# Folding the transform along d, and moving the w_out conversion into attention, in an attention, gated-mixture and Fourier-mixing kernel

## The chip, the cores and the metric

The kernel runs on one core of a Trainium2 chip. The metric is the device time of one execution in microseconds (us). Engines are called TensorE (PE), VectorE (DVE), ScalarE (ACT), GpSimd (POOL) and SyncE (SP, which only issues DMAs here).

## The reference

Three stages follow each other, for a batch of 2, 768 positions and 8 heads of 64 (512 features):

```
scores = where(bucket(q) == bucket(k), q @ k.T / 8, -1e9)   # buckets: sign bits of q @ proj
x      = softmax(scores) @ v                                # joined to 2 x 768 x 512
gate   = sigmoid(causal convolution of x over 5 positions, by feature)
x      = (gate * (x @ w_val)) @ w_out
mixed  = real(fft(fft(x, axis=1), axis=2))                  # along the sequence, then along d
u      = x + mixed
out    = u + relu(layernorm(u) @ w_ch1) @ w_ch2
```

The weights of the last two stages arrive as 64-bit floats and are read as pairs of 32-bit words.

## The kernel before

Products are kept near float32 precision by splitting each operand into a high and a low part (fp32r) and adding three products, high·high, high·low and low·high. A weight in 64 bits is first turned into such parts by `from64` (L125 to L164): five or six elementwise steps on VectorE and two on ScalarE, 512 columns at a time.

**Attention** (L230 to L819) runs over 8 pairs of heads (p), 12 steps each (i), n = 12 p + i, in the order of one hand-written loop. Each step places scores, softmax, transposes and products with v on TensorE, and beside them preparatory work: the placement of the next pair's q and k by DMA into the buffers q2 and k2, the normalization of the pair before, the conversion of one 256-column half of w_val per pair (`val_weights`, L681, whose intermediates lie in PSUM), and the convolution of finished x on GpSimd (`conv_pool`, L209, in `conv_tmp`). x is stored transposed in xT, one tile per batch. `x_split` (L185) casts a part of it to its high half on ScalarE and subtracts for the low half, on GpSimd by default. At the end of the loop value products (`val_matmul`, L194: 12 matmuls of 384 columns for a tile c of batch b and sequence half a) start: "early" tiles for (0, 0), then "late" ones for (0, 1). `gate` (L205) multiplies a value tile on VectorE with the sigmoid of the convolution.

**Mixing** (L886 to L1075) is what the change rewrites. It first does the 8 value tiles of batch 1 (`val`, L942). In program order between them stands the conversion of w_out, `run(wo[c])` at L960, four calls on 512 columns each, from a load of w_out that is issued behind the last outputs of attention (L910). The convolution of the last feature chunk (1, 3) is on GpSimd, and that of (1, 2) on VectorE (`conv_dve`, L219, at the end of attention).

Gated values g are folded along the sequence by `even_odd` (L926): VectorE adds or subtracts position j and 768 − j (gt), ScalarE casts the high part gh (L929) and GpSimd subtracts for the low part gl (L930). s = 0 is the even, s = 1 the odd part. Then:

- L974: w_out (high and low) is transposed on TensorE, 32 transposes.
- L984: w_out times the DFT table along d (`wide`, cosines and sines, 258 columns each) gives wah and wal: 96 matmuls of 258 columns.
- L1015: gh and gl times wah and wal give ah and al, the transform along d of the block's input x: 84 matmuls of 258 columns for each batch.
- `own` (L1032): gh and gl times w_out itself, 12 matmuls of 512 columns for each of 6 row tiles a batch. Both this and L1015 go through `gmm`, whose matmul is L1003.
- `mixed` (L1037, L1049): the transform along the sequence of ah and al by the tables seq and odd.
- `total` (L1054) adds own and mixed, where the columns from 257 on are the mirrored ones of 255 down to 1; GpSimd adds and subtracts even and odd totals to u (L1073), `center` takes off the mean (VectorE, L863), `u_transpose` (L877, matmul L880) makes the input of the channel stage, and `channel_split` (L857) converts w_ch1 and w_ch2 for it.

**The channel stage** (L1081 to L1163) is a loop of matmuls, L1109 and L1121.

The pool of q2 and k2 is closed with attention. All order is program order on each engine; semaphores join the engines, and a PSUM bank is reused in the order in which its pool gives it out.

Of the kernel before, what the change touches and what calls it, by code (L numbers as in the profile page):

```python
# [10 lines left out]
F32 = mybir.dt.float32  # L11
# [88 lines left out]
def block_kernel(  # L100
# [118 lines left out]
    def conv_dve(c, i):  # L219

        x, dst = xT[1], g[1][:, c, :]
        if i == 0:
            nc.vector.tensor_scalar_mul(dst, x[:, c, 0:S], cwt[:, 0, c : c + 1])
        for kk in (1, 2) if i == 0 else (3, 4):
            nc.vector.scalar_tensor_tensor(
                dst, x[:, c, kk : kk + S], cwt[:, kk, c : c + 1], dst, op0=ALU.mult, op1=ALU.add
            )


    def attention(es):  # L230
        ap1 = pool(es, "ap1")
        ap2 = pool(es, "ap2", 2)
        ap3 = pool(es, "ap3")
# [50 lines left out]
        q2 = [ap3.tile([P, 2, S], F32R, name=f"q2_{i}") for i in range(NBUF)]  # L284
        k2 = [ap3.tile([P, 2, S], F32R, name=f"k2_{i}") for i in range(NBUF)]
# [388 lines left out]
        wv_raw, wv_e = {}, {}  # L674
# [6 lines left out]
        def val_weights(i):  # L681

            c, h = divmod(i, 2)
            cs = slice(h * DM // 2, (h + 1) * DM // 2)
            n = DM // 2
            words = wv_raw[i].bitcast(I32).rearrange("p (n two) -> p n two", two=2)
            lo, hi = words[:, :, 0], words[:, :, 1]
            t = psm.tile([P, 2 * n], F32, tag="m", name="cvp")
            a, g = (t[:, x * n : (x + 1) * n].bitcast(I32) for x in range(2))

# [7 lines left out]
            def step2():  # L698
                nc.scalar.activation(a, a, AF.Relu, scale=8.0, bias=col[:, 3:4])
                e = ap1.tile([P, n], I32, tag="cve", name="cv", bufs=1)  # L700
                nc.vector.scalar_tensor_tensor(a, hi, -(2 ** 31), a, op0=ALU.bitwise_and, op1=ALU.bitwise_or)
                nc.vector.tensor_scalar(e, a, -(2 ** 23), None, op0=ALU.bitwise_and)
                wv_e[i] = e

            def step3():
                nc.vector.scalar_tensor_tensor(
                    wvl[:, c, cs], g, 2.0 ** -35, wv_e[i].bitcast(F32), op0=ALU.mult, op1=ALU.mult
                )

            def step4():  # L710
                nc.scalar.copy(wvh[:, c, cs], a.bitcast(F32))
# [4 lines left out]
        convs = [(b, c, i) for b, c in pairs[: NPR - 2] for i in range(9)]  # L716
        start()
        NT = 12 * NPR
        for n in range(NT + 2):
# [43 lines left out]
            if n == NT - 1:  # L763
# [5 lines left out]
                for c in range(NC):  # L769
                    x_split(0, 1, c)  # L770
# [18 lines left out]
            for _ in range(5 * n // 6 - 5 * (n - 1) // 6):  # L789
                if convs and n < NT and n >= 12 * (4 * convs[0][0] + convs[0][1]) + 22:  # L790
# [11 lines left out]
            if n >= NT:  # L802
                conv_dve(2, n - NT)
                sigmoid(0, 2 * (n - NT))
                sigmoid(0, 2 * (n - NT) + 1)
                if n > NT:
                    for c in range(NC):
                        gate(0, 0, c, tail[c])
        xsplit[1, 0] = xsplit[0, 0]
        late = []  # L810
        for c in range(NC):
            x_split(1, 0, c, nc.vector)
# [5 lines left out]
        for c in range(NC):  # L818
            gate(0, 1, c, late[c])  # L819

# [65 lines left out]
    def mixing(es):  # L886
        mp = pool(es, "mp")
        ps = pool(es, "psx", 8, psum=True)

        def psum():  # L890
            return ps.tile([P, 512], F32, tag="ps", name="ps")

        woh = mp.tile([P, NC, DM], F32R, name="woh")
        wol = mp.tile([P, NC, DM], F32R, name="wol")
        wah = mp.tile([P, NC, 2, NL], F32R, name="wah")
        wal = mp.tile([P, NC, 2, NL], F32R, name="wal")


        ep = pool(es, "ep", 2)
        seq = ep.tile([P, 2, 2, 3, HS], F32R, name="seq", bufs=1)  # L900
        odd = ep.tile([P, 2, P], F32R, name="odd", bufs=1)
        vs = ExitStack()
        vp = pool(vs, "vp", side="right")
        conv_tmp = xT[0].rearrange("p c t -> p (c t)")[:, :S]
        gts = [ep.tile([P, HS], F32, name=f"gt{i}", bufs=1) for i in range(4)]
        rs = ExitStack()
        rp = pool(rs, "rp")
        raws = [rp.tile([P, DM], I64, name=f"wor{c}") for c in range(NC)]
        for c in range(NC):
            nc.sync.dma_start(raws[c], w_out[c * P : (c + 1) * P, :])  # L910
        toh = vp.tile([P, NC, DM], F32R, name="toh")
        tol = vp.tile([P, NC, DM], F32R, name="tol")
        wide = vp.tile([P, 2, NC, 2 * NL], F32R, name="wide")
        xsplit[1, 1] = tuple(vp.tile([P, NC, HS], F32R, name=f"xs{i}") for i in "hl")


        gh, gl = {}, {}

        def parts_tiles(b, pl):
            for s in range(2):  # L920
                gh[b, s] = pl.tile([P, NC, HS], F32R, tag=f"gh{s}", name="gh", bufs=1)
                gl[b, s] = pl.tile([P, NC, HS], F32R, tag=f"gl{s}", name="gl", bufs=1)

# [15 lines left out]
        wo = [from64(rp, raws[c], woh[:, c, :], wol[:, c, :], half=True) for c in range(NC)]  # L939
# [6 lines left out]
        nc.gpsimd.dma_start(wide, t_wide)  # L946
        for i in range(6):
            conv_pool(1, 3, i, conv_tmp)
        for c in range(NC):
            x_split(1, 1, c)  # L950
        for c in range(3):
            sigmoid(1, c)
        for i in range(6, 9):
            conv_pool(1, 3, i, conv_tmp)
        nc.gpsimd.dma_start(seq, t_seq)
        nc.gpsimd.dma_start(odd, t_odd)
        for c in range(NC):
            val(0, c)
        for c in range(NC):
            run(wo[c])  # L960
            val(1, c)
            if c == 3:
                sigmoid(1, 3)
                nc.scalar.activation(warm, warm, AF.Sqrt)
            gate(1, 0, c, pvs[0, c])
        for c in range(NC):
            gate(1, 1, c, pvs[1, c])


        for c in range(NC):  # L970
            for i, (w, to) in enumerate(((woh, toh), (wol, tol))):
                pw = psum()
                for m in range(NC):
                    nc.tensor.transpose(pw[:, m * P : (m + 1) * P], f32(w)[:, m, c * P : (c + 1) * P], ident)  # L974
                nc.scalar.copy(to[:, c, :], pw)
        rs.close()
        pp = pool(es, "pp")
        parts_tiles(0, pp)
        for i, (m, part) in enumerate((m, part) for part in range(2) for m in range(NC)):
            pa = psum()  # L980
            n = 0
            for w, x in ((toh, 0), (toh, 1), (tol, 0)):
                for c in range(NC):
                    nc.tensor.matmul(  # L984
                        pa[:, :NL], w[:, c, m * P : (m + 1) * P], wide[:, x, c, part * NL : (part + 1) * NL],
# [216 lines left out]
```

## Time and profile before

| what | us |
|---|---|
| median of 3 runs (657.67 to 661.81) | 659.42 |
| the profiled execution | 658.59 |
| its span in the trace | 656.8 |
| TensorE busy | 636.2 |
| VectorE busy | 454.3 |
| ScalarE busy | 357.6 |
| GpSimd busy | 275.2 |

The span is what the trace covers, from the first instruction to the last; the execution's time has 1.8 us around it. Busy shares average over stages with different limits, so the reading goes by stretches. Attention lasts to about 257 us, mixing to 380.3, the channel stage to the end.

### The profile page before, as it was taken

How to read it: one execution, taken by the hardware profiler on the slowest of the kernel's cores; microseconds unless marked ns; L12 is line 12 of the kernel's file. 1: busy time of each engine (PE TensorE's matmuls, PEld its weight loads, DVE VectorE, ACT ScalarE, POOL GpSimd, SP SyncE). 2: the span in 40 equal slices, each digit the busy share in tenths (PEclk: the TensorE clock that was granted, in tenths of full speed). 3: DMA queues.
4: the chain of work that ended last, by engine and by line, in shares of the span. 5: the costliest groups of instructions: out<-in, count | busy, mean ns of one | idle time of the engine just before them, and what ended most of it. 6: DMA issues, size and time to landing. Idle time of an engine off the chain costs nothing.

```text
span 656.8 us, 10829 instructions
## 1 busy us (share of the span) xinstructions
PE 636.2 (97%) x3954; PEld 597.1 (91%) x3954; DVE 454.3 (69%) x832; ACT 357.6 (54%) x707; POOL 275.2 (42%) x285
## 2 busy tenths in 40 slices
PE   7999999999999999969999989999999999999997
PEld 6899999999999999869989878999999899999996
DVE  4998999999898987987756478899886511111113
ACT  5888989888798996355313345555665211111110
POOL 7132578788788698925531343333332000000000
PEclk9999999999999999979999999999999999999999
DMA  6957465675755303450000123444441100000002
GB/s 157 202 124 169 128 160 126 145 181 132 188 130 132 92 17 114 153 216 1 1 1 1 54 76 129 128 129 129 128 130 64 70 26 1 0 1 1 0 1 96
DMA packets 54061, 61.32 MB, mean 93 GB/s; under 512 B 28936, under 2 KB 42332, under 8 KB 53752
## 3 DMA queue, kind: packets, MB, share of 16 engines
q1 hardware_dynamic: 53272, 56.02, 32.1%
q0 software_dynamic: 432, 4.60, 1.9%
q8 instruction: 31, 0.51, 0.3%
q14 instruction: 22, 0.18, 0.1%
q10 hardware_dynamic: 304, 0.01, 0.0%
HBM read 35.04 MB, written 3.15 MB: 58 GB/s over the span
## 4 chain that ended last, share of the span: by engine, by line
PE 80%; DVE 11%; POOL 3%; issue 2%; ACT 1%; SPq 1%; DMA 1%; DVEq 0%; POOLq 0%; ACTq 0%
PE pf L1109 19%; PE acc L1121 19%; PE sp L469 8%; PE ps L1003 8%; PE op L529 8%; PE ptp L506 7%; PE ps L1049 2%; PE bp L346 2%; DVE ptl L518 1%; DVE sd L481 1%; PE ptp L601 1%; DVE cv L149 1%; DVE cv L146 1%; PE ps L974 1%; POOL g L217 1%
## 5 line engine op out<-in xcount | busy, mean ns | idle before, releaser
L1121 PE MATMUL acc<-w,hid 128*128 128x512 f32 x576 | 137.1, 390 | 0.0
L1121 PEld LDWEIGHTS acc<-w,hid 128*128 128x128 f32 x576 | 107.4, 188 | 19.8
L1112 DVE SCALAR_TENSOR_TENSOR hid<-pf,hid 128x384 fp32r<-128x384 f32 x60 | 32.2, 555 | 120.0 <-ACT hid L1111 120.0
L481 DVE TENSOR_SCALAR_CACHE_REDUCE sd<-sp 128x768 f32<-128x768 f32 x96 | 91.0, 948 | 16.1 <-PE sp L469 15.2
L518 DVE TENSOR_TENSOR ptl<-ptp,pth 128x768 fp32r<-128x768 f32 x96 | 91.4, 952 | 5.9 <-ACT pth L514 5.9
L1109 PE MATMUL pf<-uth,w 128*128 128x384 f32 x480 | 94.7, 338 | 0.2 <-POOL w L155 0.2
L514 ACT CAST pth<-ptp 128x768 fp32r<-128x768 f32 x96 | 77.3, 805 | 31.0 <-PE ptp L506 13.6
L469 PE MATMUL sp<-k,q 128*128 128x384 f32 x384 | 90.8, 358 | 3.0 <-DVE sd L481 1.7
L488 ACT ACTIVATE sd<-sd,nm 128x768 f32<-128x768 f32 x96 | 90.7, 944 | 2.7 <-DVE sd L481 2.7
L1111 ACT ACTIVATE hid<-pf 128x384 fp32r<-128x384 f32 x60 | 28.0, 488 | 113.9 <-PE pf L1109 113.9
L1109 PEld LDWEIGHTS pf<-uth,w 128*128 128x128 f32 x480 | 85.6, 187 | 3.0 <-POOL w L155 0.5
L155 POOL TENSOR_TENSOR w<-cv 128x512 fp32r<-128x512 f32 x32 | 41.4, 1293 | 107.9 <-DVE cv L150 95.5
L506 PE MATMUL ptp<-ident,sd 128*128 128x128 f32 x576 | 78.6, 273 | 0.2 <-ACT sd L488 0.2
L529 PE MATMUL op<-ptl,v 128*128 128x256 f32 x288 | 73.8, 285 | 0.0
L529 PE MATMUL op<-pth,v 128*128 128x256 f32 x288 | 73.8, 283 | 0.0
L469 PEld LDWEIGHTS sp<-k,q 128*128 128x128 f32 x384 | 62.3, 189 | 6.3 <-DVE sd L481 4.1
L506 PEld LDWEIGHTS ptp<-ident,sd 128*128 128x128 f32 x576 | 65.8, 141 | 1.0 <-ACT sd L488 0.5
L547 POOL TENSOR_TENSOR xm<-xc,xs 64x256 f32<-64x256 f32 x48 | 36.1, 751 | 67.8 <-ACT sd L488 31.6
L142 ACT ACTIVATE cv<-cv,col 128x512 int32<-128x512 int32 (+1 forms) x37 | 26.5, 716 | 57.6 <-DVE cv L139 57.6
L529 PEld LDWEIGHTS op<-ptl,v 128*128 128x128 f32 x288 | 54.7, 190 | 0.9 <-issue 0.2
L529 PEld LDWEIGHTS op<-pth,v 128*128 128x128 f32 x288 | 54.6, 190 | 0.0
L1109 PE MATMUL pf<-utl,w 128*128 128x384 f32 x240 | 52.1, 338 | 0.0
(222 smaller groups left out, 1118.2 us busy)
## 6 DMA issues: line engine op xcount, KB each, us to landing
raw<-in_moe_w_ch_dram SPq DMA_DIRECT2D x32, 512.0 KB, 3.7
q<-ht SPq DMA_DIRECT2D x30, 192.0 KB
k<-ht SPq DMA_DIRECT2D x30, 192.0 KB, 3.1
rqk<-in_q_dram SPq DMA_DIRECT2D x16, 192.0 KB, 3.6
rqk<-in_k_dram SPq DMA_DIRECT2D x16, 192.0 KB, 4.5
rv<-in_v_dram SPq DMA_DIRECT2D x8, 384.0 KB, 3.3
out_dram<-o SPq DMA_DIRECT2D x12, 256.0 KB, 2.1
xs<-xc SPq DMA_DIRECT2D x47, 64.0 KB, 1.9
```

The costliest lines, as they stand in the source:

```text
L155: nc.gpsimd.tensor_tensor(dst_l, fold(g.bitcast(F32)), fold(e.bitcast(F32)), op=ALU.mult)
L469: nc.tensor.matmul(sp[:, a, :HS], q2[i][:, m, qi * P : (qi + 1) * P], k2[i][:, m, a * HS : (a + 1) * HS], start=m == 1, stop=m == 0,)
L481: nc.vector.tensor_scalar(sd[n].rearrange("p (a c) -> p a c", a=2), sp[:, :, :HS], CLAMP, None, op0=ALU.min, op1=ALU.min, accum_out=st[p][ ...
L488: nc.scalar.activation(sd[n], sd[n], AF.Exp, bias=st[p]["nm"][:, i : i + 1], scale=-1.0, accum_out=st[p]["sums"][:, i : i + 1],)
L506: nc.tensor.transpose(tp[:, r // 3, c0 : c0 + P], sd[n][:, r * P : (r + 1) * P], ident)
L514: nc.scalar.copy(p_parts(n)[0], tp)
L518: nc.vector.tensor_tensor(lo, tp, f32(ho), op=ALU.subtract)
L529: nc.tensor.matmul(po[kb], v3[:, r, c0 : c0 + P], pt[kb][x][:, r, :], start=r == 0 and x == 0, stop=r == R - 1 and x == 1,)
L547: add[kb] = lambda: nc.gpsimd.tensor_tensor(st[p]["xm"][mr, blk * QB : (blk + 1) * QB], xc[mr, :], xs[mr, :], op=ALU.add)
L1003: nc.tensor.matmul(dst, x[:, c, m * P : (m + 1) * P], w(c), start=n == 0, stop=n == 3 * NC - 1)
L1109: nc.tensor.matmul(pf[:, :HS], w[:, c, :], x[:, c, cs], start=n == 0, stop=n == 3 * NC - 1)
L1121: nc.tensor.matmul(acc, x[:, ts_], w, start=f == 0 and n == 0, stop=f == NF - 1 and n == 2)
```

## The change

- The transform along d is applied to y = own(x) after it has been formed, not to w_out. VectorE folds y along d: columns d and 512 − d are added (for part 0) or subtracted (part 1), with a fold of 256 columns (`fold`). TensorE transposes the fold, 3 or 2 blocks (`turn`), ScalarE and VectorE split it into high and low parts, and `along_d` multiplies by a table of half the size (`tab`, and `first` for d = 0): 8 or 6 matmuls of 258 columns for each of the 7 parts a batch, 100 in all. L974, L984 and the narrow use of L1003 go. The 12 pairs (b, s, kt) run as passes i = 0 to 13 of one loop, with `own` of pass i, `along_d` of pass i − 2 and `turn` of pass i − 1.
- `total` adds the mixed tile from PSUM straight into y in SBUF.
- w_out is loaded in eight halves of 256 columns during pairs 6 and 7 (`out_load`) and converted by `half_weights` (the code of `val_weights`) into the buffers of q and k, whose pool stays open. Half 0 is converted in the loop, halves 1 to 7 behind it, each in a `begin` (three VectorE steps) and an `end` (ScalarE and three VectorE steps).
- `x_split(0, 0)` goes from pair 7 to pair 5; the subtraction of `x_split(0, 1)` from GpSimd to VectorE; the convolution of (1, 2) from VectorE to GpSimd; the multiplications of (1, 3) from GpSimd to ScalarE (`conv_act`). The sigmoids and gates of (0, 0) come earlier.
- The means of batch 0 (`center`) are placed in passes 8 to 10, the conversions of the first channel weights in passes 9 and 10, the transposes of u in passes 11 to 13.
- PSUM in mixing: 2 banks for `turn` and 6 for the rest, where it was one pool of 8.

The core of the diff:

```diff
-            if p == 7 and i in (1, 3, 5, 7):
+            if p == 6 and i in (2, 6):
+                out_load(i // 6)
+            if last and i == 7:
+                for x in range(2):
+                    out_load(2 + x)
+                    out_tile(x)
+                osteps = out_weights(0, "m")
+            if last and 7 <= i < 11:
+                osteps[i - 7]()
+                if i == 10:
+                    osteps[4]()
+            if p == 5 and i in (1, 3, 5, 7):
                 x_split(0, 0, i // 2)
...
+        begin(1)
+        x_high(1, 0, 0)
+        x_high(1, 0, 1)
+        begin(2)
+        end(1)
+        x_high(1, 0, 2)
+        x_high(1, 0, 3)
+        for c in range(3):
+            x_low(1, 0, c, nc.vector)
+        late_gate(0)
+        end(2)
+        begin(3)
+        x_low(1, 0, 3, nc.vector)
+        late_gate(1)
+        begin(4)
+        end(3)
+        late_gate(2)
+        end(4)
+        begin(5)
+        begin(6)
+        late_gate(3)
+        end(5)
+        end(6)
+        begin(7)
+        end(7)
...
         for c in range(NC):
             x_split(1, 1, c)
+        for c in range(NC):
+            val(0, c)
+        for c in range(2):
             sigmoid(1, c)
+            gate(1, 0, c, pvs[0, c])
+        conv_act(3)
         nc.gpsimd.dma_start(seq, t_seq)
         nc.gpsimd.dma_start(odd, t_odd)
...
+        def fold(b, s, kt, yp):
+            y = ys[b, s, kt] = m2.tile([P, DM], F32, tag="y", name="y", bufs=7)
+            nc.scalar.copy(y, yp)
+            for part in (s,) if s == 0 or kt else (0, 1):
+                fo = folds[b, s, kt, part] = m2.tile([P, 2 * P], F32, tag="fold", name="fold", bufs=2)
+                nc.vector.tensor_tensor(
+                    fo, yp[:, 1:257], y[:, 511:255:-1], op=ALU.subtract if part else ALU.add
+                )
...
+        for i in range(len(jobs) + 2):
+            if i < len(jobs):
+                yp = own(*jobs[i])
+            if i > 1:
+                for x in spans(jobs[i - 2]):
+                    if x[0] not in sums:
+                        sums[x[0]] = [m2.tile([P, 2, 4, NL], F32R, tag=y, name="a") for y in ("ah", "al")]
+                    along_d(*x)
+            if 0 < i <= len(jobs):
+                for x in spans(jobs[i - 1]):
+                    turn(*x)
+            if i == 7:
+                both(0, 0)
+                both(0, 1)
+            if i < len(jobs):
+                fold(*jobs[i], yp)
```

How the order moves at three places. Names: `wor` is a raw piece of w_out, `cvp` its intermediates in PSUM, `qk` its converted parts; `xl`, `xsh` and `xsl` are parts of x of batch 1; g_73 and g_74 are the gates of batch 0 and 1.

VectorE behind the last step of attention, before:

```order
L189 TENSOR_TENSOR xl<-xT_78,xh 128x384 x4
L207 TENSOR_TENSOR g_73<-late,g_73 128x384 x4
L139 TENSOR_SCALAR cv<-wor_3859 128x512
L145 TENSOR_SCALAR cv<-wor_3859 128x512
L146 SCALAR_TENSOR_TENSOR cv<-wor_3859,cv 128x512
```

and after, around the third and fourth of the late gates:

```order
L216 TENSOR_TENSOR g_73<-late,g_73 128x384
L746 SCALAR_TENSOR_TENSOR cvp<-wor,cvp 128x256
L747 TENSOR_SCALAR cv<-cvp 128x256
L750 SCALAR_TENSOR_TENSOR qk<-cvp,cv 128x256
L738 TENSOR_SCALAR cvp<-wor 128x256
L739 TENSOR_SCALAR cvp<-wor 128x256
L742 SCALAR_TENSOR_TENSOR cvp<-wor,cvp 128x256
L738 TENSOR_SCALAR cvp<-wor 128x256
L739 TENSOR_SCALAR cvp<-wor 128x256
L742 SCALAR_TENSOR_TENSOR cvp<-wor,cvp 128x256
L216 TENSOR_TENSOR g_73<-late,g_73 128x384
```

The four late gates, which stood together ahead of all of w_out, now have halves of it between them.

GpSimd in the first part of mixing, before:

```order
L189 TENSOR_TENSOR xsl<-xT_78,xsh 128x384 x4
L217 TENSOR_TENSOR g_74<-g_74,xT_72 128x768
L215 TENSOR_SCALAR xT_72<-xT_78,cwt 128x768
L217 TENSOR_TENSOR g_74<-g_74,xT_72 128x768
L955 DMA seq<-const_seq_dram 128x4608
L956 DMA odd<-const_odd_dram 128x256
L930 TENSOR_TENSOR gl<-gt_3852,gh 128x384
```

and after:

```order
L1029 MEMSET first 1x258
L194 TENSOR_TENSOR xsl<-xT_78,xsh 128x384 x4
L235 TENSOR_TENSOR g_74<-g_74,xT_72 128x768 x4
L1038 DMA seq<-const_seq_dram 128x4608
L1039 DMA odd<-const_odd_dram 128x256
L1013 TENSOR_TENSOR gl<-gt_3958,gh 128x384
```

All four additions stand behind the subtractions xsl now, where two of four did.

ScalarE at the same place, before:

```order
L188 CAST xh<-xT_78 128x384 x4
L188 CAST xsh<-xT_78 128x384 x4
L192 ACTIVATE g_74<-g_74 128x768 x3
L142 ACTIVATE cv<-cv,col 128x512
L162 CAST woh<-cv 128x512
```

and after:

```order
L753 CAST qk<-cvp 128x256
L745 ACTIVATE cvp<-cvp,col 128x256
L753 CAST qk<-cvp 128x256
L189 CAST xsh<-xT_78 128x384 x4
L201 ACTIVATE g_74<-g_74 128x768 x2
L233 ACTIVATE g_74<-xT_78,cwt 128x768
L233 ACTIVATE xT_72<-xT_78,cwt 128x768 x4
```

The casts xsh, which stood ahead of w_out's steps, now stand behind the last of them.

## Rows read from the trace of the kernel before

**Rows 1.** The page's first part: busy us, share of span, instructions.

```profile
PE 636.2 (97%) x3954; PEld 597.1 (91%) x3954; DVE 454.3 (69%) x832; ACT 357.6 (54%) x707; POOL 275.2 (42%) x285
```

**Rows 2.** Table by stretch: bounds, length, busy by engine, granted clock, DMA share, GB/s.

```profile
210.00:256.90 46.90, 46.03 (x342) 45.05 (x341) 39.17 (x66) 40.27 (x82) 38.28 (x38) 1.00 0.21 50
...
288.00:294.00 6.00, 3.83 (x18) 3.84 (x19) 4.96 (x10) 5.03 (x9) 0.00 (x0) 0.50 0.95 355
...
307.30:380.30 73.00, 72.59 (x471) 65.90 (x470) 41.70 (x93) 22.58 (x51) 26.07 (x23) 1.00 0.05 15
```

**Rows 3.** TensorE's timeline, 256 to 381 us: start, length, instruction, [idle before].

```profile
256.88 0.86 PE L199 MATMUL late<-x,wvh 128*128 128x384 f32 x4
...
265.21 0.86 PE L199 MATMUL ps<-xh,wvh 128*128 128x384 f32 x4
...
286.51 0.33 PE L974 MATMUL ps<-ident,woh 128*128 128x128 f32 x1 [2.31 <-ACT woh L162]
290.17 0.48 PE L974 MATMUL ps<-ident,woh 128*128 128x128 f32 x1 [3.32 <-ACT woh L162]
...
295.17 0.60 PE L974 MATMUL ps<-ident,wol 128*128 128x128 f32 x4
295.52 1.40 PE L984 MATMUL ps<-wide,toh 128*128 128x258 f32 x8
...
307.28 0.53 PE L1003 MATMUL ps<-wah,gh 128*128 128x258 f32 x3
...
333.00 1.10 PE L1003 MATMUL ps<-wol,gh 128*128 128x512 f32 x4
...
335.80 1.10 PE L1003 MATMUL ps<-wol,gh 128*128 128x512 f32 x4
...
380.29 1.56 PE L1109 MATMUL acc<-uth,w 128*128 128x384 f32 x8
```

**Rows 4.** VectorE by line to 257 us, first and last of six w_val steps.

```profile
L693 DVE TENSOR_SCALAR cvp<-wvr 128x256 int32<-128x256 int32 x8 | 3.4, 428 | 0.3
...
L706 DVE SCALAR_TENSOR_TENSOR wvl<-cvp,cv 128x256 fp32r<-128x256 int32 x8 | 3.3, 407 | 0.0
```

**Rows 5.** VectorE's timeline, 261 to 368 us.

```profile
261.49 3.29 DVE L189 TENSOR_TENSOR xl<-xT,xh 128x384 fp32r<-128x384 f32 x4
264.70 1.93 DVE L207 TENSOR_TENSOR g<-late,g 128x384 f32<-128x384 f32 x4
...
329.38 0.69 DVE L866 BATCH_NORM_STATS2 st<-u 128x6 f32<-128x512 f32 x1 [1.41 <-POOL u L1073]
...
330.80 0.68 DVE L866 BATCH_NORM_STATS2 st<-u 128x6 f32<-128x512 f32 x1
...
365.30 0.42 DVE L139 TENSOR_SCALAR cv<-raw 128x512 int32<-128x512 int32 x1
...
367.41 0.43 DVE L150 TENSOR_SCALAR cv<-cv 128x512 int32<-128x512 int32 x1
```

**Rows 6.** ScalarE by line, 200 to 400 us.

```profile
L192 ACT ACTIVATE g<-g 128x768 f32<-128x768 f32 x8 | 6.3, 840 | 0.0
...
L188 ACT CAST xsh<-xT 128x384 fp32r<-128x384 f32 x4 | 1.8, 512 | 0.0
...
L699 ACT ACTIVATE cvp<-cvp,col 128x256 int32<-128x256 int32 x2 | 0.9, 460 | 0.0
```

**Rows 7.** GpSimd by line, 240 to 400 us.

```profile
L930 POOL TENSOR_TENSOR gl<-gt,gh 128x384 fp32r<-128x384 f32 x16 | 17.7, 1125 | 22.9 <-ACT gh L929 22.9
...
L189 POOL TENSOR_TENSOR xsl<-xT,xsh 128x384 fp32r<-128x384 f32 x4 | 4.9, 1255 | 0.0
...
L217 POOL TENSOR_TENSOR g<-g,conv_tmp 128x768 f32<-128x768 f32 x2 | 3.7, 1867 | 0.0
...
L955 POOL DMA_DIRECT2D seq<-const_seq_dram x1 | 0.6, 587 | 0.0
```

**Rows 8.** VectorE by line, 200 to 400 us.

```profile
L1017 DVE TENSOR_TENSOR al<-ps,ah 128x258 fp32r<-128x258 f32 x14 | 5.9, 419 | 2.1 <-ACT ah L1016 2.1
```

More of the change, by code (lines that the diff above doesn't have):

```diff
@@ L887, in mixing, with psum @@
         mp = pool(es, "mp")
[L888 to L914, printed above, removed]
+        pw = pool(es, "psw", 2, psum=True)
+        ps = pool(es, "psx", 6, psum=True)
+        def psum(pl=ps):
+            return pl.tile([P, 512], F32, tag="ps" if pl is ps else "pw", name="ps")
+        tab = mp.tile([P, 2, 2, 2, NL], F32R, name="tab")
+        first = mp.tile([P, NL], F32R, name="first")
+        seq = mp.tile([P, 2, 2, 3, HS], F32R, name="seq")
+        odd = mp.tile([P, 2, P], F32R, name="odd")
         gh, gl = {}, {}
@@ L955, in mixing @@
+        conv_act(3)
         nc.gpsimd.dma_start(seq, t_seq)
         nc.gpsimd.dma_start(odd, t_odd)
[L957 to L960, printed above, removed]
+        for c in range(2):
             val(1, c)
[L962 to L966, printed above, removed]
-            gate(1, 1, c, pvs[1, c])
[L970 to L980, printed above, removed]
+        even_odd((0, 0, 0), (0, 1, 0))
+        sigmoid(1, 2)
+        gate(1, 0, 2, pvs[0, 2])
+        for c in range(2):
+            gate(1, 1, c, pvs[1, c])
+        for c in range(2, NC):
+            val(1, c)
+        for c in range(1, NC):
+            even_odd((0, 0, c), (0, 1, c))
+        even_odd()
@@ L981, in mixing, with own @@
+        sigmoid(1, 3)
+        nc.scalar.activation(warm, warm, AF.Sqrt)
+        gate(1, 1, 2, pvs[1, 2])
+        for a in range(2):
+            gate(1, a, 3, pvs[a, 3])
+        def own(b, s, kt):
+            yp = psum()
             n = 0
[L982 removed]
+            for x, w in ((gh[b, s], wo_h), (gh[b, s], wo_l), (gl[b, s], wo_h)):
                 for c in range(NC):
                     nc.tensor.matmul(
[L985 to L986 removed]
+                        yp, x[:, c, kt * P : (kt + 1) * P], w[c], start=n == 0, stop=n == 3 * NC - 1
@@ new lines, in turn @@
+        def turn(b, s, kt, part):
+            n = 2 if part else 3
+            pt = psum(pw)
+            for i, x in enumerate([folds[b, s, kt, part][:, i * P : (i + 1) * P] for i in range(2)]):
+                nc.tensor.transpose(pt[:, i * P : (i + 1) * P], x, ident)
+            if n == 3:
+                nc.tensor.transpose(pt[:, 2 * P : 3 * P], ys[b, s, kt][:, 0:P], ident)
+            fh, fl = turned[b, s, kt, part] = [
+                m2.tile([P, 3, P], F32R, tag=f"f{x}", name="ft", bufs=2)[:, :n] for x in "hl"
+            ]
+            src = pt[:, : n * P].rearrange("p (n t) -> p n t", n=n)
+            nc.scalar.copy(fh, src)
+            nc.vector.tensor_tensor(fl, src, f32(fh), op=ALU.subtract)
@@ new lines, in mixing, with along_d @@
+        sums = {}
+        def along_d(b, s, kt, part):
+            fh, fl = turned[b, s, kt, part]
+            ops = [(x[:, i, :], tab[:, part, w, i, :]) for x, w in ((fh, 0), (fh, 1), (fl, 0)) for i in range(2)]
+            if part == 0:
+                ops += [(x[:, 2, :], first) for x in (fh, fl)]
+            pa = psum()
+            for n, (x, w) in enumerate(ops):
+                nc.tensor.matmul(pa[:, :NL], x, w, start=n == 0, stop=n == len(ops) - 1)
+            ah, al = sums[b]
+            slot = kt if part == s else 3
+            nc.scalar.copy(ah[:, part, slot, :], pa[:, :NL])
+            nc.vector.tensor_tensor(al[:, part, slot, :], pa[:, :NL], f32(ah)[:, part, slot, :], op=ALU.subtract)
@@ new lines, in both @@
+        def both(b, kt):
+            pm = [mixed(b, s, kt) for s in range(2)]
+            for s in range(2):
+                total(b, s, kt, pm[s])
+            for t, op in ((kt, ALU.add), (3 + kt, ALU.subtract)):
+                nc.gpsimd.tensor_tensor(u[b][:, t, :], ys[b, 0, kt], ys[b, 1, kt], op=op)
+        rs.close()
+        vs.close()
+        xs.close()
+        m2 = pool(es, "m2")
+        gts = [m2.tile([P, HS], F32, name=f"gt{i}") for i in range(2)] * 2
+        parts_tiles(1, m2)
```

260 lines of the change are left out of this document (135 added, 125 removed).

## The prediction

> **What bounds the kernel now.** I read the page first. TensorE is busy for 636.2 of 656.8 us [rows 1], so time can only go where TensorE's own work shrinks or where one of its few waits ends. The table by stretch shows where those are [rows 2]: TensorE works 46.03 of the last 46.9 us of attention and 72.59 of the 73.0 us from 307.3 to 380.3; between 288 and 294 it works 3.83 of 6.0 us, at a granted clock of 0.50, the lower of its two levels (1.2 GHz). TensorE's timeline says why [rows 3]: the first transposes of w_out (L974) wait 2.31 and then 3.32 us for the converted weights, then run slowly. So the stretch to work out is from 256.88 (first late value matmul, "zero" below) to 380.29 (first channel matmul): 123.4 us.
>
> From the same rows I take prices. A value tile of 12 matmuls: (265.21 − 256.88) / 4 = 2.08 us. Four transposes at full clock: 295.52 − 295.17 = 0.35, so 0.09 each. The 96 narrow matmuls (258 columns) of L984: 307.28 − 295.52 = 11.8, so 0.12 each. Twelve wide ones (512 columns): 335.80 − 333.00 = 2.80.
>
> **What goes on TensorE.** Out: 32 transposes (2.8 us), the 96 matmuls of L984 (11.8), 168 narrow matmuls of L1003 (20.2). In: 100 narrow matmuls (12.0) and 36 transposes of folds (3.2). Both kernels have the 144 wide ones (33.5), the 132 of the mixing along the sequence (15.8), the 24 transposes of u (2.2) and the 12 value tiles (25.0). Net 34.8 − 15.2 = 19.6 us less work. The waits of 2.31 and 3.32 go as well, and 3.83 busy us at half clock give back 1.9. Were nothing late in their place, that is 19.6 + 5.6 + 1.9 = 27 us. I don't expect it, since the order of the other engines changes too.
>
> **What is late next, first: VectorE after attention.** Halves 1 to 7 of w_out now stand on VectorE among the gates. A half is six VectorE steps of 407 to 428 ns [rows 4], so 1.25 us to begin it and 1.25 to end it. The second value tile of batch 1 needs a PSUM bank which the last late gate frees. Ahead of that gate stand, from half 1 on, 6 begins and 4 ends (12.5 us), four subtractions (3.29) and four gates (1.93, [rows 5]). Half 1 itself starts when the last copy of attention frees its bank, about 0.95. So the tile starts near 19.0; TensorE would come to it at 8.33 + 2.08 = 10.4. Nothing covers these 8.6 us: all later tiles are behind it.
>
> **Second: ScalarE, then GpSimd.** The high parts of the last quarter of x (four casts in 1.8 us, [rows 6]) stood before the w_out conversion; now they stand behind half 7. VectorE needs for ends 5 and 6 and half 7 another 5.0 us, and the ScalarE steps between (0.46 each, [rows 6]) come uncovered in the last half, so half 7 is done at about 25.3 and the casts end at 27.1. GpSimd's four subtractions took 4.9 us, 1.26 each [rows 7]; the first can follow the first cast, so they now end near 31. Value tiles 5 to 8 end near 31.5 + 3 × 2.08 = 37.7. Behind the subtractions GpSimd's queue holds four additions of 768 columns (1.87 each, 7.5), two DMA issues (0.59 each, 1.2) and then the eight low parts gl of batch 0 (1.125 each, 9.0, all [rows 7]). Its last gl is done at 31.0 + 7.5 + 1.2 + 9.0 = 48.7. ScalarE's new products for those additions are no row of before; between its 768-column sigmoid (0.84, [rows 6]) and a GpSimd addition of that size (1.87); at either end the first is done before GpSimd is free, and only at the upper can the fourth be late, by 1 us at most: I add nothing.
>
> The first two wide groups (5.6 us) need all of gh and gl of batch 0: eight of twelve matmuls can go ahead, the last four of the second follow the last gl, so they end at about 50.8. TensorE sits still from 37.7 to about 45, longer than before, so I charge the clock as rows 2 show it: 1.9 us again, and 0.4 (my estimate) while it comes back. They end at 53.1. Before, the narrow L1003 began at 50.4.
>
> **Third: from there to the channel stage.** TensorE's work left is 10 wide groups (28.0), 12.0 narrow, 5.4 transposes, 15.8 mixing: 61.2 us. VectorE has 1 fold, 1 or 2 low parts and 1 or 2 differences a pass, each 0.42 (258 columns, [rows 8]) to 0.49 (a gate's 384 columns). In passes 8 to 10 it also gets the means (two tiles of u at 330.80 − 329.38 = 1.42 each, 2.8, [rows 5]) and in 9 and 10 the channel weights (365.30 to 367.84, 2.5 us, [rows 5]). Passes 8 to 12 sum to 4.6 + 7.1 + 6.5 + 2.8 + 2.2 = 23.2 us of VectorE against 19.3 us of TensorE (pass 9: 0.84 differences, 0.49 low part, 0.42 fold, 2.8 and 2.5, against a wide group, 14 narrow matmuls and three transposes), since passes 12 and 13 have no wide group left to fill. TensorE waits the difference, 3.9, and about 1.7 for the last link (ScalarE's copy and VectorE's difference): 5.6 us. 3.9 and 7.5 are the ends. A further 1.5 for the clock behind such a wait (bounds 0 and 3.8) and 1 for the link ahead of the last mixing. Sum: 53.1 + 61.2 + 5.6 + 1.5 + 1.0 = 122.4, against 123.4: **1.0 less**.
>
> **Attention.** Half 0 (2.5 us) and the subtractions of x (3.2) go to VectorE, the convolution steps there (7.9) leave; GpSimd gets 12.0 us of convolution and loses about 10 of subtractions. TensorE has 0.87 us of waits in the last 46.9 us [rows 2], so there is nothing to gain. Against it stand eight DMAs of 256 KB put on SyncE's queue ahead of normalized outputs and of q and k for the next pair, and more on ScalarE in pair 5. No row shows that wait: 0 if it stays hidden, 4.5 if each delayed placement is passed on in full at 0.5 us per issue. I take 1.5, nearer the end at which TensorE shows no wait.
>
> The sum is −1.0 + 1.5 = **+0.5 us**. The profiled execution took 658.6 us (span 656.8 and 1.8 around it), so the changed kernel comes to 659.1; the median of the runs is 0.8 above that execution, hence about **660 us**: no difference that can be told.
>
> **Rivals.**
> *Faster: GpSimd is not in the way.* If gl comes as TensorE finishes the values, the wait from 37.7 to 45 and its clock loss vanish: 7.3 + 2.3 = 9.6 us, so about 650.5; with the value waits gone too (8.6, and 5.6 of the last passes), 636. For it: VectorE has little to do while GpSimd adds, and no row shows such an addition beside an idle VectorE. Against: four additions, two issues and eight gl are 17.7 us in one queue, whatever VectorE does. Chance 0.23.
> *Slower: the clock stays down in the last passes.* The place is passes 9 to 13, 16.5 us of TensorE work in bursts of 1.4 to 4.7 us with a wait of about 2 us between them. Before, waits of 2.31 and 3.32 us around a single transpose brought the clock to 0.50 [rows 2, 3]; full work followed there. If it is down for all five passes the work takes 33 us where I counted 16.5 + 5.6, so 10.9 us more: 671; for half of them, 665 to 666. It decides from the point at which the granted clock is below 0.9 in these passes. Against: no wait but those two cost any clock before. Chance 0.15.
> The Trainium skill (TensorE: Matmul & The Clock Gate, section "HAM oscillation — how this bites in real kernels") tells of just this: short bursts of matmuls with waits between them, each beginning at the lower clock. By that page alone the 671 would be likelier than I make it; rows 2 agree that a wait lowers the clock, and none shows a row of them.
> *Slower: the weights' DMAs hold up attention.* The 4.5 of above in full, and products on ScalarE at their upper end: 4 us more, 664. Chance 0.10.
> *The change does nothing*, as the first two waits grow to just what TensorE saves: this is the forecast, chance 0.52.
>
> **The numbers.** About 1% (6.6 us) is what a measurement of this kernel tells from no change. Adding the ends of the forecast's own terms gives 651 to 667. The faster rival's 650.5 and the slower one's partial forms widen this to 648 to 669. Faster by over 1%: 0.24 (the first rival, and the lowest edge of the forecast). Slower by over 1%: 0.22 (the clock, part of the DMA case, the forecast's upper edge). Within: 0.54.
>
> **What would show it right or wrong.** In the changed kernel's profile: the value tile's wait for VectorE's gate near 11 us after zero, some 5 us or more long; value tiles in batch 1's second half waiting for GpSimd's subtractions; a wait of about 7 us ahead of the first wide group, released by gh or gl, with the clock at 0.5 behind it; a narrow stretch from there of about 70 us; waits for VectorE in the last passes. If the first wide group starts within 2 us of the last value tile, the second step is wrong and the kernel is faster. If the granted clock in the last passes is below 0.9, the slower rival holds. If zero itself lies more than 3 us later than 256.88, attention was mis-sized.

## The result and the profile after

The changed kernel takes 662.40 us (median of 20 runs), the kernel before 658.25 beside it: a ratio of 1.0054 [1.0039, 1.0068], 0.5% slower. The interval lies above 1, so this is more than noise, and it is within the 1% that the prediction called no change. Its profiled execution took 661.64 us with a span of 659.9, 3.1 more than before.

The page's first part for the changed kernel, columns as in [rows 1]:

```profile
PE 626.3 (95%) x3794; PEld 584.2 (89%) x3794; DVE 461.0 (70%) x875; ACT 361.1 (55%) x718; POOL 273.9 (42%) x287
```

TensorE is busy 9.9 us less than in [rows 1], although 19.6 us of its work went: most of the rest came back as matmuls at the lower clock. And the span grew, so the gain went into waits. Those that TensorE has between 150 and 400 us, the three largest and the small one for xsl (engine, what it was doing, what released it: total us, times, longest):

```profile
PE ps L1064 <- ACT gh L1012: 8.1, 3, 4.0
PE ps L208 <- DVE g L216: 7.5, 2, 4.1
PE ps L1104 <- ACT ft L1092: 5.1, 2, 4.5
...
PE ps L208 <- POOL xsl L194: 0.5, 1, 0.5
```

Of the three only the wait for gh was there before, with 0.4 us. L208 is the value matmul, L1064 the wide groups of own, L1104 `along_d`. The table by stretch, columns as in [rows 2], shows what they did to the clock:

```profile
210.00:257.10 47.10, 46.55 (x344) 45.37 (x343) 40.56 (x75) 40.92 (x83) 37.64 (x36) 1.00 0.32 83
...
270.00:295.20 25.20, 21.34 (x97) 20.52 (x96) 18.97 (x38) 12.29 (x23) 9.88 (x8) 0.75 0.09 37
295.20:312.20 17.00, 8.91 (x25) 6.16 (x25) 13.50 (x20) 5.89 (x10) 11.77 (x11) 0.70 0.58 208
312.20:360.00 47.80, 47.80 (x293) 42.58 (x292) 29.55 (x71) 16.39 (x39) 15.50 (x14) 1.00 0.00 1
360.00:369.00 9.00, 3.90 (x25) 2.87 (x23) 7.76 (x19) 4.88 (x11) 2.04 (x2) 0.94 0.24 67
369.00:375.00 6.00, 6.00 (x29) 6.00 (x30) 4.46 (x9) 3.66 (x8) 0.51 (x1) 0.52 0.20 76
```

Attention (first row) is as full as in [rows 2]. Between 312.2 and 360 TensorE never stops and has its full clock: the fold itself runs as intended. The losses lie in the three stretches with clocks of 0.75, 0.70 and 0.52, each holding or following one of the waits. TensorE's timeline, as [rows 3], gives the places:

```profile
257.08 0.86 PE L208 MATMUL late<-x,wvh 128*128 128x384 f32 x4
...
269.70 1.62 PE L208 MATMUL ps<-xh,wvh 128*128 128x384 f32 x4 [4.12 <-DVE g L216]
271.12 1.48 PE L208 MATMUL ps<-xh,wvl 128*128 128x384 f32 x4
...
277.23 1.65 PE L208 MATMUL ps<-xh,wvh 128*128 128x384 f32 x4 [3.35 <-DVE g L216]
...
295.20 0.40 PE L1064 MATMUL ps<-qk,gh 128*128 128x512 f32 x1
297.79 0.50 PE L1064 MATMUL ps<-qk,gh 128*128 128x512 f32 x1 [2.19 <-ACT gh L1012]
302.29 0.80 PE L1064 MATMUL ps<-qk,gh 128*128 128x512 f32 x1 [4.01 <-ACT gh L1012]
304.98 2.50 PE L1064 MATMUL ps<-qk,gh 128*128 128x512 f32 x5 [1.89 <-ACT gh L1012]
...
312.22 0.38 PE L1085 MATMUL ps<-ident,fold 128*128 128x128 f32 x2
...
368.96 1.66 PE L1104 MATMUL ps<-tab,ft 128*128 128x258 f32 x6 [4.50 <-ACT ft L1092]
...
383.32 1.55 PE L1229 MATMUL acc<-uth,w 128*128 128x384 f32 x8
```

From zero (257.08) to the first channel matmul (383.32) it is 126.2 us, where before had 123.4 [rows 3]. The account: 27.1 us were to be gained (work, waits and clock, as in the prediction) and 1.8 more from small waits for GpSimd (1.4) and gh (0.4), which it left out; with the 2.8 of the longer stretch, 31.7 us have to be found. The four waits above are 21.2. The rest is the clock: of the value tiles, two take 4.2 and 4.0 us in place of 2.08 and a third of the next 1.28 for 0.69, together 4.6; the last 21 wide matmuls take 7.24 us (304.98 to 312.22) for 21 × 2.80 / 12 = 4.9, so 2.3; 6 us at 0.52 cost 0.48 × 6 = 2.9. Sum 31.0: nearly all is found.

What the wide groups wait for stands on GpSimd's timeline (start, length, instruction, idle before):

```profile
284.65 3.93 POOL L194 TENSOR_TENSOR xsl<-xT,xsh 128x384 fp32r<-128x384 f32 x4 [15.61 <-ACT xsh L189]
289.01 8.15 POOL L235 TENSOR_TENSOR g<-g,xT 128x768 f32<-128x768 f32 x4 [0.44 <-ACT xT L233]
297.12 0.58 POOL L1038 DMA_DIRECT2D seq<-const_seq_dram  x1
297.69 0.54 POOL L1039 DMA_DIRECT2D odd<-const_odd_dram  x1
298.24 2.90 POOL L1013 TENSOR_TENSOR gl<-gt,gh 128x384 fp32r<-128x384 f32 x3
301.78 5.85 POOL L1013 TENSOR_TENSOR gl<-gt,gh 128x384 fp32r<-128x384 f32 x5 [0.65 <-ACT gh L1012]
```

GpSimd sits idle for 15.6 us, then does everything in one line, and the last gl is done at 307.6. VectorE's timeline shows a second effect, which the prediction did not have:

```profile
288.91 0.15 DVE L1019 TENSOR_TENSOR gt<-g 128x1 f32<-128x1 f32 x1
...
289.45 1.80 DVE L1019 TENSOR_TENSOR gt<-g 128x1 f32<-128x1 f32 x1
...
292.19 1.49 DVE L216 TENSOR_TENSOR g<-ps,g 128x384 f32<-128x384 f32 x3 [0.93 <-ACT g L201]
...
295.43 1.75 DVE L1019 TENSOR_TENSOR gt<-g 128x1 f32<-128x1 f32 x1
...
297.57 3.58 DVE L1019 TENSOR_TENSOR gt<-g 128x1 f32<-128x1 f32 x1
```

A sum of one column takes 0.15 us while GpSimd is idle and 1.75, 1.80 or 3.58 while it works: the sum of 295.43 ends at 297.18, with GpSimd's last addition (297.16), that of 297.57 at 301.15, with the third gl (301.14). So sums and low parts hold each other up, and gh, which ScalarE casts from the sums, is late as well. It is gh that TensorE waits for last in this stretch, until 304.98; the last gl, at 307.6, comes in time for the matmuls behind. The gates at 292.19, which read one of their two inputs from PSUM, are not held: three take 1.49 us beside the additions, and four took 1.93 in [rows 5].

### The profile page after: what moved, and what is told of

Its sections match the earlier page's. It is cut to its first block, busy times and chain, and to the rows that moved or that the text cites. A ratio compares the mean times of both kernels' runs of the same rounds, so it can differ in the third digit from the quotient of the medians.

```text
span 659.9 us, 10600 instructions
## 1 busy us (share of the span) xinstructions
PE 626.3 (95%) x3794; PEld 584.2 (89%) x3794; DVE 461.0 (70%) x875; ACT 361.1 (55%) x718; POOL 273.9 (42%) x287
## 4 chain that ended last, share of the span: by engine, by line
PE 80%; DVE 12%; ACT 3%; issue 2%; POOL 1%; DMA 1%; SPq 0%; ACTq 0%; DVEq 0%; POOLq 0%
PE pf L1229 19%; PE acc L1241 19%; PE sp L485 9%; PE op L545 9%; PE ptp L522 8%; PE ps L1064 5%; PE ps L1124 2%; PE bp L362 2%; PE ps L1104 2%; DVE sd L497 1%; PE ptp L617 1%; DVE gt L1019 1%; DVE ptl L534 1%; PE early L208 1%; DVE xl L194 1%
## 5 line engine op out<-in xcount | busy, mean ns | idle before, releaser
L497 DVE TENSOR_SCALAR_CACHE_REDUCE sd<-sp 128x768 f32<-128x768 f32 x96 | 90.9, 948 | 15.6 <-PE sp L485 14.9
L485 PE MATMUL sp<-qk 128*128 128x384 f32 x384 | 90.9, 358 | 3.0 <-DVE sd L497 1.9
L485 PEld LDWEIGHTS sp<-qk 128*128 128x128 f32 x384 | 62.4, 189 | 6.7 <-DVE sd L497 4.3
L145 ACT ACTIVATE cv<-cv,col 128x512 int32<-128x512 int32 (+1 forms) x33 | 23.6, 715 | 53.6 <-DVE cv L142 53.6
L226 POOL TENSOR_TENSOR g<-g,conv_tmp 128x768 f32<-128x768 f32 x28 | 52.4, 1870 | 1.3
```

The lines of the kernel that those rows point to most:

```text
L226: nc.gpsimd.tensor_tensor(dst, dst, tmp, op=ALU.add)
L485: nc.tensor.matmul(sp[:, a, :HS], q2[i][:, m, qi * P : (qi + 1) * P], k2[i][:, m, a * HS : (a + 1) * HS], start=m == 1, stop=m == 0,)
L497: nc.vector.tensor_scalar(sd[n].rearrange("p (a c) -> p a c", a=2), sp[:, :, :HS], CLAMP, None, op0=ALU.min, op1=ALU.min, accum_out=st[p][ ...
```

## The experiments

My theory was the prediction's: three chains (VectorE's gates behind the halves, GpSimd's queue ahead of gl, VectorE's steps in the last passes) take back what the fold saves. The rivals: that TensorE would be held elsewhere once a chain is broken, or that the clock alone is the loss. All edits are to the changed kernel. Each run had runs of the kernel before beside it on the same chip; where two kernels are compared below, it is by their ratios to it, times 658.25 us.

**Late gates ahead of halves 2 to 7.**

```diff
+        x_low(1, 0, 3, nc.vector)
+        for c in range(1, NC):
+            late_gate(c)
         end(2)
         begin(3)
...
```

> The changed kernel with the four late gates of batch 0 ahead of halves 2 to 7 of w_out on VectorE. My theory (the chain through ScalarE's casts behind half 7 and GpSimd's queue decides when the wide groups start): TensorE's waits for gates (4.1 and 3.4 us) shrink to about 1 and 0, but the value tiles of the second half still wait for GpSimd's subtractions, so that wait grows by as much; the first wide group starts within 1.5 us of 295.2 and the time stays within 2 us of the changed kernel's 662.4. The rival (each wait of TensorE costs for itself): 7 us faster, about 655.

Measured: 664.02 us, ratio 1.0075 [1.0049, 1.0101]. TensorE's waits:

```profile
PE ps L208 <- ACT xsh L189: 9.3, 1, 9.3
PE ps L1063 <- ACT gh L1011: 7.6, 3, 4.0
```

The waits for gates fall from 7.5 to 2.8 us, and one of 9.3 for the casts xsh takes their place. The first wide group starts at 297.42, 2.2 us later, where I allowed 1.5; the time stayed within the 2 us expected. The first wait was covering the second chain.

**Casts and low parts xsl ahead of halves 2 to 7**, with buffers of their own for ScalarE's products.

```diff
+        for c in range(NC):
+            x_high(1, 1, c)
         for c in range(3):
             x_low(1, 0, c, nc.vector)
...
         for c in range(NC):
-            x_split(1, 1, c)
+            x_low(1, 1, c)
```

> The changed kernel with the four casts of the last quarter of x ahead of halves 2 to 7 on ScalarE (their target is the memory of x of batch 0, so ScalarE's convolution products get a buffer of their own). My theory: GpSimd's subtractions end near 274 where they ended at 288.6, the value tiles end about 2 to 3 us earlier, but the additions still wait for ScalarE's products behind half 7, which move by the casts' 1.8 us only: 1 to 3 us faster. The rival (the casts' place alone makes the 12 us between value tiles and wide groups): 6 us or more faster.

Measured: 659.51 us, 1.0017 [1.0003, 1.0032]. GpSimd's timeline:

```profile
268.88 3.89 POOL L194 TENSOR_TENSOR xs<-xT,xs 128x384 fp32r<-128x384 f32 x4
287.22 7.80 POOL L237 TENSOR_TENSOR g<-g,ct 128x768 f32<-128x768 f32 x4 [14.45 <-ACT ct L235]
```

The subtractions end 15.8 us earlier, but the additions start only 1.8 us earlier: they wait for ScalarE's products, which still stand behind half 7. Taking xsl out of the line saves 0.0037 of 658.25, 2.4 us, no more.

**Low parts gl of batch 0 on VectorE.**

```diff
-                nc.gpsimd.tensor_tensor(gl[b, s][:, c, :], gt, f32(gh[b, s])[:, c, :], op=ALU.subtract)
+                (nc.gpsimd if b else nc.vector).tensor_tensor(gl[b, s][:, c, :], gt, f32(gh[b, s])[:, c, :], op=ALU.subtract)
```

> The changed kernel with the eight low parts gl of batch 0 on VectorE, not behind the additions in GpSimd's queue. My theory (GpSimd's queue): the last gl comes 2 to 4 us before 307.6 and the time falls by 2 to 5 us. The rival (VectorE's one-column steps held up while GpSimd adds, 1.75 to 3.6 us each, decide): gl then waits behind these on VectorE, under 2 us gained, or a loss of up to 2.

Measured: 660.03 us, 1.0023 [1.0008, 1.0037], 2.0 better than the changed kernel. VectorE's timeline:

```profile
295.20 4.00 DVE L1013 TENSOR_TENSOR gl<-gt,gh 128x384 fp32r<-128x384 f32 x2
...
300.32 1.10 DVE L1013 TENSOR_TENSOR gl<-gt,gh 128x384 fp32r<-128x384 f32 x2
```

Two low parts take 1.10 us on a free VectorE and 4.00 beside GpSimd's additions. The 2.0 us lie at the lower end of my theory and just beyond the rival's 2, so the time alone does not decide; the rows show the rival's hold at work. Leaving GpSimd's queue gains little for a step that GpSimd also holds up.

**Channel weights converted two passes earlier.**

```diff
+            elif i == 6:
+                channel_split(0)
             elif i == 7:
                 both(0, 2)
+                channel_split(1)
...
-                if i > 8:
-                    channel_split(i - 9)
```

> The changed kernel with the conversions of the first two channel weights in passes 6 and 7 of the mixing loop, not 9 and 10. My theory (VectorE has more to do than TensorE in the last passes): the waits of 0.6 and 4.5 us in passes 11 and 12 fall to under 1.5 us together and the clock no longer falls to 0.5 between 369 and 375 (about 2.7 us): 5 to 8 us faster, about 656. The rival (VectorE is just as full in passes 6 and 7, so the wait only moves): within 2 us of 662.4.

Measured: 655.07 us, 0.9944 [0.9924, 0.9965], 7.2 better than the changed kernel. The table by stretch:

```profile
360.00:369.00 9.00, 8.03 (x60) 7.32 (x58) 8.79 (x22) 4.98 (x12) 0.00 (x0) 1.00 0.01 2
369.00:375.00 6.00, 6.00 (x53) 6.00 (x51) 4.08 (x11) 0.91 (x2) 1.65 (x2) 1.00 0.00 0
```

The wait of 5.1 us in the last passes falls to 1.0 and the granted clock stays at 1.00 where it was 0.52, which is 4.1 + 2.9 = 7.0 us. VectorE was full there: the means and two conversions stood ahead of the steps that `along_d` waits for.

**The convolution of (1, 3) on GpSimd, in its idle stretch.**

```diff
-        for x in convs:
+        for x in convs + [(1, 3, i) for i in range(9)]:
             conv_pool(*x, conv_tmp)
...
-        conv_act(3)
```

> The changed kernel with the last convolution chunk (1, 3) wholly on GpSimd, in the 15.6 us in which it stands idle behind attention, and not as ScalarE products and GpSimd additions behind its subtractions. My theory (these four additions are the second wait, both as 8.2 us in GpSimd's queue ahead of gl and as the holder-up of VectorE's sums): the last gl near 300, the first two wide groups end near 302 to 303 where they ended at 312.2, 8 to 11 us faster, about 652. The rival (VectorE's sums stand behind gates of batch 1 that wait for TensorE's value tiles, additions or not): 2 to 4 us faster.

Measured: 653.49 us, 0.9916 [0.9892, 0.9940], 9.1 better. GpSimd's and then TensorE's timeline:

```profile
286.21 3.92 POOL L194 TENSOR_TENSOR xsl<-xT,xsh 128x384 fp32r<-128x384 f32 x4 [3.41 <-ACT xsh L189]
...
294.47 7.26 POOL L1013 TENSOR_TENSOR gl<-gt,gh 128x384 fp32r<-128x384 f32 x6 [1.23 <-ACT gh L1012]
```

```profile
296.72 0.86 PE L1063 MATMUL ps<-qk,gh 128*128 128x512 f32 x3
299.04 1.44 PE L1063 MATMUL ps<-qk,gh 128*128 128x512 f32 x5 [1.46 <-ACT gh L1012]
...
304.05 0.38 PE L1084 MATMUL ps<-ident,fold 128*128 128x128 f32 x2
```

GpSimd now does ScalarE's five multiplications as well, and the kernel is faster: the last gl is done at 301.7 in place of 307.6 (although zero, the first late value matmul, lies 1.2 us later in this execution), one wait of 1.5 us is left of 8.1, and the wide groups run at the full clock. This is the second chain, shown. The edit also takes five products off ScalarE, where VectorE's third gate of batch 1 waited 0.93 us for the sigmoid behind them; the runs do not separate that part.

**Filling the waits for gh** with 20, 38 and 18 transposes of the identity, whose results nothing reads.

```diff
+        FILL = {1: 20, 2: 38, 3: 18}
...
+                    if (b, s, kt) == (0, 0, 0) and n in FILL:
+                        dummy = psum(pw)
+                        for _ in range(FILL[n]):
+                            nc.tensor.transpose(dummy[:, :P], ident, ident)
```

> The changed kernel with 20, 38 and 18 idle transposes on TensorE in its waits for gh (2.2, 4.0 and 1.9 us) ahead of the second, third and fourth matmul of the first wide group. They compute nothing that is used. My theory of the clock (the fall to 0.50 between 300 and 310 is the wait's own price, 5.8 busy us at half speed): the granted clock stays 1.00 there and the time falls by 1.5 to 3 us. The rival (the wide groups are held by gl's arrival, so their speed is hidden): within 1 us of 662.4.

Measured: 659.98 us, 1.0012 [0.9998, 1.0026], 2.8 better than the changed kernel. The table by stretch:

```profile
290.00:300.00 10.00, 9.98 (x66) 9.58 (x66) 9.09 (x11) 4.65 (x8) 9.58 (x7) 1.00 0.22 65
300.00:312.00 12.00, 11.77 (x79) 10.26 (x78) 9.96 (x17) 5.52 (x10) 8.27 (x8) 1.00 0.63 242
```

With TensorE kept busy the clock stays at 1.00 through the same waits. So the clock is worth some 3 us there, and the rest of the 9.1 lies in the waits: the clock alone is not the loss.

**Both: convolution ahead and weights earlier.**

> Both edits together: the last convolution chunk ahead on GpSimd, and the first two channel weights converted in passes 6 and 7. If the waits are two separate ones, as my theory has it, the gains add: 15 to 18 us faster than the changed kernel, about 645, and 2% faster than before. If the second only takes over what the first leaves (the rival: VectorE is the bound from the values to the end of mixing), 8 to 11 us.

Measured: 646.27 us, 0.9807 [0.9781, 0.9833]. That is 16.3 us better than the changed kernel, the sum of the two gains, 9.1 and 7.2: the second and third chains are independent.

**Everything ahead**: the gates, casts, xsl and the convolution of (1, 3) ahead of halves 2 to 7, the sums of batch 0 ahead of most gates of batch 1, weights in passes 6 and 7.

```diff
+        for c in range(NC):
+            x_split(1, 1, c)
+        for i in range(9):
+            conv_pool(1, 3, i, conv_tmp)
...
+        for c in range(1, NC):
+            late_gate(c)
         end(2)
...
         for c in range(1, NC):
             even_odd((0, 0, c), (0, 1, c))
         even_odd()
+        nc.gpsimd.dma_start(seq, t_seq)
+        nc.gpsimd.dma_start(odd, t_odd)
...
+        for c in range(NC):
+            gate(1, 1, c, pvs[1, c])
```

> All that the theory asks for: late gates ahead of halves 2 to 7, casts and subtractions of the last quarter of x and the last convolution chunk ahead of them too (GpSimd's idle stretch), the sums of batch 0 ahead of most gates of batch 1, channel weights in passes 6 and 7. The first two wide groups then end near 296 (they ended at 312.2), bounded by half 7 of w_out at 284 and 8 us of gl behind it, and the last passes lose no clock: 21 to 25 us faster than the changed kernel, about 639. Rival (TensorE's value tiles, still held by PSUM banks until VectorE has done half 7): 650.

Measured: 643.69 us, 0.9767 [0.9740, 0.9794], the fastest, 2.3% below the kernel before. It is 2.6 us better than the last one, where I expected some 7, and the first two wide groups end at 301.33, not near 296. TensorE's timeline:

```profile
285.73 1.49 PE L208 MATMUL ps<-xs,wvh 128*128 128x384 f32 x4 [3.23 <-DVE g L216]
...
294.77 1.44 PE L1061 MATMUL ps<-qk,gh 128*128 128x512 f32 x5 [2.18 <-ACT gh L1019]
```

The last value tiles now wait for PSUM banks that the gates of batch 1 free, and these gates stand behind half 7 on VectorE. This is the rival's mechanism: the halves are still in the way, only later.

**The one-column sum with a single tensor operand.**

```diff
-                nc.vector.tensor_tensor(gt[:, 0:1], g[b][:, c, 0:1], g[b][:, c, HS : HS + 1], op=op)
+                nc.vector.tensor_scalar(gt[:, 0:1], g[b][:, c, 0:1], g[b][:, c, HS : HS + 1], None, op0=op)
```

> The kernel of the run before with everything ahead, and there the one-column sum of VectorE (position 0 of each gt) taken with its second operand as a scalar per partition, so that this step has one tensor input. In that run these steps took 0.15 us where GpSimd was idle and 0.94 to 0.97 beside gl on GpSimd. If the hold comes with two tensor inputs in SBUF, all of them take 0.15 to 0.2; but the sum of 383 columns behind each has two such inputs and can take over the hold, so the last gh comes between 0 and 4 us earlier and the time falls by 0 to 2 us, about 643. The rival (any short VectorE step waits while GpSimd works, whatever its inputs): they still take about 0.95.

Measured, on top of the last kernel: 643.96 us, 0.9770 [0.9742, 0.9798], no change. VectorE's timeline:

```profile
290.68 0.20 DVE L1026 TENSOR_SCALAR gt<-g 128x1 f32<-128x1 f32 x1
290.80 1.24 DVE L1025 TENSOR_TENSOR gt<-g 128x383 f32<-128x383 f32 x1
```

Each one-column step takes 0.20 to 0.21 us beside GpSimd's low parts now, where 0.94 to 0.97 stood. The sum of 383 columns behind it, 0.54 before, takes 1.22 to 1.24 instead: the hold passes to the next step that reads two tensors.

**The fold alone**: w_out loaded and converted in mixing by 512 columns, as before the change, and the gates and casts ahead.

```diff
-        begin(1)
...
-        end(7)
...
+        raws = [rp.tile([P, DM], I64, name=f"wor{c}") for c in range(NC)]
+        for c in range(NC):
+            nc.sync.dma_start(raws[c], w_out[c * P : (c + 1) * P, :])
+        wo = [from64(rp, raws[c], wo_h[c], wo_l[c], half=True) for c in range(NC)]
...
+        for c in range(NC):
+            run(wo[c])
             val(1, c)
```

> One part of the change alone: the fold along d with all its passes, but w_out loaded and converted in mixing by 512 columns on VectorE, between the value tiles of batch 1, as before; the late gates and the casts of the last quarter of x again stand ahead of it. My theory (the loss lies in where the halves of w_out were put, not in the fold): no wait for gates, gh and gl ready near 300, the first two wide groups end near 304, the rest takes the 71 us of the changed kernel: about 654, 4 to 6 us faster than before. The rival (the fold itself gives nothing since VectorE has its steps to do in each pass): 658 or more.

Measured: 659.45 us, 1.0015 [0.9999, 1.0030]: my expectation of 654 fell. TensorE's and VectorE's timelines:

```profile
295.21 0.79 PE L1032 MATMUL ps<-qk,gh 128*128 128x512 f32 x1 [8.20 <-ACT gh L987]
...
309.58 0.38 PE L1053 MATMUL ps<-ident,fold 128*128 128x128 f32 x2
```

```profile
290.72 0.69 DVE L160 SCALAR_TENSOR_TENSOR qk<-cv 128x512 fp32r<-128x512 int32 x1
...
293.99 0.55 DVE L993 TENSOR_TENSOR gt<-g 128x383 f32<-128x383 f32 x1
```

TensorE waits 13.1 us for gh in all, 8.2 of it once, since VectorE's sums start at 294, behind the conversion. Before, the 96 narrow matmuls of L984 lay just there, from 295.5 to 307.3 [rows 3], and covered sums, casts and low parts. The fold takes away the cover with the work; this is read from the places in the two timelines. There are also 3.3 us of waits for gates, where I expected none, and the 5.1 us in the last passes, so TensorE waits as long as in the changed kernel (21.5 us against 21.2). So the halves, with the order of gates and sums around them, cost 2.6 us net (1.0054 against 1.0015); the rest of the missing gain is not theirs. Part of it is the third chain, which the earlier conversion of the channel weights would take away here too: by its 7.2 us the fold alone would come to about 652, an estimate that no run tests.

## Why the prediction was right

The forecast, 660.0 with no difference that can be told, came out at 662.4, and by its own mechanism in the main; step by step:

- **Attention**: +1.5 predicted, +0.2 measured (zero at 257.08). The DMAs stayed hidden, although their share rose from 0.21 [rows 2] to 0.32; this term was sized 1.3 too high. The rival in which they cost 4.5 falls.
- **First step, gates behind the halves**: the second value tile of batch 1 starts 20.1 us after zero, 19.0 predicted (its terms add to 18.7), released by the gate named. The wait came as two, 4.1 and 3.4 us, with the lower clock between, in place of one of 8.6: the first tile of batch 1 already waited for a late gate, which the prediction did not have.
- **Second step**: half 7 done at 26.7 after zero (25.3 predicted), casts 28.7 (27.1), subtractions 31.5 (31.0), value tiles 38.1 (37.7), last gl 50.5 (48.7), two wide groups 55.1 (53.1). The mis-sized term is VectorE's sums, counted as free while GpSimd adds: they took up to 3.58 us and made gh late, 2.0 us at the end of the step. The prediction had the last gl end it; in the trace it was gh, cast from the sums. It called VectorE almost idle while GpSimd adds; the few sums that it had there were enough. ScalarE's products, put at nothing, cost 0.4 us ahead of the first addition.
- **Third step**: 71.1 us against 69.3. The waits are 5.1 for 5.6, and the clock took 2.9 where 1.5 stood. The 1.0 for a link ahead of the last mixing did not come: TensorE does not wait there. In its place TensorE's own work is 1.9 us longer than the 61.2 counted (66.0 busy, less the 2.9). Some 0.8 of this are nine wide groups of 2.88 us, where 2.80 was counted; the rest stays unassigned.
- **The slower rival**, the clock down in all of the last passes: it is down from 369 to 375 alone, behind the wait of 4.5 us. By the prediction's own sign, a clock below 0.9, the rival holds for these 6 us, and they cost 2.9 of the 10.9 that all five passes would have cost.
- **The faster rival**, GpSimd not in the way, 650.5: it did not happen by itself, and the kernel with the convolution ahead shows what it is worth, 653.5.

Two errors of +2.0 and +1.8 and one of −1.3 make the 2.5 us by which the profiled execution (661.64) lies above the 659.1 forecast for it. The sum stood on the net of two large numbers, 27 us freed and as much given back, so a total that is off by 2.5 us owes something to luck: an error of a tenth in either number would have been as large. Of the three places at which the time is given back, the experiments price two (9.1 and 7.2 us); that these add to 16.3 was not in the prediction. The first, the gates, has no price of its own: taken away alone it gained nothing, and the fastest kernel still waits 6.0 us for gates. Not tried: the fold with w_out converted as before the change and the other placements of the fastest kernel.

## What to carry to other kernels

Work taken off the busiest engine is also cover taken from the chains that ran beside it: follow those chains to the first matmul that needs them before counting a gain, and move the work of the idle engines into the place where they idle (9.1 us here by one such move). Where such a kernel shows no gain, look for the few new waits and repair each; here two small moves turned +0.5% into −1.9%. A step put between others on a queue delays all that stands behind it, so short steps that free banks or feed other engines go first; this pays only once no other chain waits behind (here gates first, alone, gained nothing).

## What the runs showed of the hardware

VectorE's timeline of the kernel before, beside GpSimd's low parts:

```profile
299.19 0.15 DVE L936 TENSOR_TENSOR gt<-g 128x1 f32<-128x1 f32 x1
...
300.08 0.97 DVE L936 TENSOR_TENSOR gt<-g 128x1 f32<-128x1 f32 x1
```

A VectorE step that reads two tensors from SBUF can be held until GpSimd's step ends, however short it is: one column took 0.15 us free, 0.94 to 0.97 beside low parts of 384 columns, and 1.75 to 1.80 beside additions of 768. With one tensor operand it took 0.20 in the same place. Not every such step is held: the sum of 383 columns that follows a held column took its free 0.54 us in the changed kernel, and the low part beside it 1.38 in place of 0.99. The kernel before had the hold too, but L984 covered it. The Trainium skill (SBUF — State Buffer, section "SBUF: two separate sides") says that the two engines share a port pair which one of them holds for its whole instruction, and that two SBUF inputs on VectorE need it. The trace agrees for most steps, and for the gates with one input in PSUM, which were not held. The step of 3.58 us outlasted one instruction: it began while GpSimd issued its DMAs and ended with the third of three low parts in a row. Why, no run shows.

The table by stretch of the changed kernel, around the waits for gh:

```profile
300.00:310.00 10.00, 5.82 (x13) 4.25 (x14) 7.37 (x13) 5.38 (x9) 6.98 (x7) 0.50 0.58 227
310.00:320.00 10.00, 10.00 (x54) 8.41 (x53) 6.37 (x17) 4.19 (x10) 3.41 (x4) 1.00 0.00 0
```

The granted clock is 0.50, the lower level of 1.2 GHz, behind waits of 2.19 and 4.01 us around single matmuls, and stays at 1.00 when idle transposes fill those waits, which gave back 2.8 us.
